# Windowed attention of chunks 2 to 8 on 64x64 TensorE tiles, in plain float32, with the transposes first

## The chip, the cores and the metric

The kernel runs on one core of one Trainium2 chip. The metric is the device time of one execution in microseconds: the median of three runs. One more execution was recorded by the hardware profiler, and every duration below comes from that record. The engines are TensorE (PE for its matmuls, PEld for its weight loads), VectorE (DVE), ScalarE (ACT), GpSimd (POOL) and SyncE (SP, which issues most of the DMAs).

## What is computed

Three stages follow one another: attention with a causal window of 128 and a linear bias, a dense gated feed-forward, and a mixture of eight experts that takes the best expert of each token.

```python
# q, k, v: [4, 8, 576, 64] float32; window = 128
scores = q @ k.T / sqrt(64)
rel = pos[:, None] - pos[None, :]
scores = where((rel >= 0) & (rel < 128), scores - slope[h] * abs(rel), -1e9)
attn = softmax(scores);  x = (attn @ v) as [2304, 512]
h = x @ w_in;  y = (h * clip(h + 3, 0, 6) / 6) @ w_out        # 512 -> 2048 -> 512
e = argmax(cosine(y, expert_emb) / tau)                        # 8 experts
out = gate * relu(y @ w1[e]) @ w2[e]                           # 512 -> 1024 -> 512
```

A query sees its own key and the 127 before it, so 64 queries that start at a multiple of 64 need 192 keys at most: the 128 before the block and the 64 of the block.

## The kernel before

The 2304 tokens are cut into nine **chunks** of 256. Attention is done in **units** of one chunk and one pair of heads, 36 in all. Chunks 0 and 1 (class `Early`) are worked off in a list that `plan()` writes ahead of time, together with the preparation of the feed-forward weights. Chunks 2 to 8 are 28 units of class `Unit`, and they are the ones that change.

What a `Unit` does, in order: `load` and `load_v` fetch keys, queries and values (SP's DMAs); `transpose_qk` turns keys and queries on DVE so that the 64 features of head 0 lie in partitions 0 to 63 and those of head 1 in 64 to 127; `split_qk` makes of each a high and a low part in the type fp32r (ACT and DVE); `scores` (L621) multiplies in three passes (high x high, high x low, low x high), for 128 queries by 256 keys at a time, one head in the upper half of TensorE's rows and one in the lower; `soften` adds the bias from `table`, takes the largest and the exponential; `normalise` divides; `flip_p` (L683) transposes the weights on TensorE against `ident`; `unload_p` copies them from PSUM (ACT) and splits them with two masks (POOL) into the part of the own key block and that of the block before; `values` (L723) multiplies by `vr` into one PSUM tile `acc`, head 0 in the left half of TensorE's columns, head 1 in the right; `keep_x` splits `acc` into the fp32r pair `xs` that the feed-forward reads. Where a chunk crosses the end of a sequence (every 576 tokens), the blocks have 64 rows, and there are more of them.

TensorE, ACT, DVE and SP work their instructions off in program order, and that order is set by numbers: `at(step, fn)` hangs a function on a step, and all are emitted by step (those of one step as they were entered). A group of attention work stands at `group(n)`, between two blocks of the feed-forward: the values of unit n-2, the flips of unit n-1 and the scores of unit n, in this order. `gemm1` (L750) and `gemm2` (L793) of the feed-forward lie around it, 24 matmuls of 128x128 by 256 columns and 12 by 512, all fp32r in three passes. PSUM has eight banks, handed out by the tile framework (`bank`).

At the very start POOL makes constants in program order: `whole` and `table` (the bias, L172 to L181), some others, and `units_of` (L215), the scale of the queries, which the first ACT instruction on queries (L439) reads.

A plain float32 matmul shows as two records in the trace, and a transpose or an fp32r matmul as one.

Of the kernel before, what the change touches and what calls it, by code (L numbers as in the profile page):

```python
# [19 lines left out]
MASKED = -1.0e32  # L20
# [37 lines left out]
P_BUFS, V_BUFS = 2, 2  # L58

# [31 lines left out]
def tile_kernel(  # L91
# [89 lines left out]
    nc.gpsimd.tensor_copy(out=table, in_=whole)  # L181

# [153 lines left out]
    def segments(c):  # L336

        qs, ks = [], []
        g, end = c * CH, (c + 1) * CH
        while g < end:  # L340
            b, s = divmod(g, S)
            n = min(S - s, end - g)
            prev = None
            if s:
                h = min(128, s)
                ks.append((b, s - h, h))
                prev = len(ks) - 1
            for o, m in runs(n):
                ks.append((b, s + o, m))
                qs.append((b, s + o, m, len(ks) - 1, prev))  # L350
                prev = len(ks) - 1
            g += n
        return qs, ks


# [170 lines left out]
    class Unit:  # L526
        def __init__(self, n):
            self.c, self.p = divmod(n, NP)
            self.h0 = 2 * self.p
            self.qs, self.ks = segments(self.c)  # L530
            self.koff = [sum(x[2] for x in self.ks[:j]) for j in range(len(self.ks) + 1)]
            self.qoff = [sum(x[2] for x in self.qs[:j]) for j in range(len(self.qs) + 1)]
            self.soff = [0]
            for _, _, m, _, prev in self.qs:
                self.soff.append(self.soff[-1] + m + (self.ks[prev][2] if prev is not None else 0))


            self.width, self.wins = {}, []
            col = 0
            for full in (True, False):  # L540
                for j, (_, _, m) in enumerate(self.ks):
                    if (m == 128) == full:
                        users = [i for i, x in enumerate(self.qs) if x[3] == j]
                        users += [i for i, x in enumerate(self.qs) if x[4] == j]
                        w = sum(self.qs[i][2] for i in users)
                        self.wins.append((j, m, col, w, users))
                        col += w
                self.width[full] = col
            self.own, self.prev = {}, {}
            for j, _, at, _, users in self.wins:  # L550
                for i in users:
                    (self.own if self.qs[i][3] == j else self.prev)[i] = at
                    at += self.qs[i][2]

            befores = {x[4] for x in self.qs}
            self.row = [128 - x[2] if j in befores else 0 for j, x in enumerate(self.ks)]
            self.even = all(x[2] == 128 and x[4] is not None and self.ks[x[4]][2] == 128 for x in self.qs)
            self.pt, self.sm, self.pp = {}, {}, {}
        def load(self):
            def get_blocks(src, blocks, off, nm):  # L560

                t = raw.tile([128, off[-1] // 32, 32], F32, tag=nm, name=nm)
                j = 0
                while j < len(blocks):
                    b, s, n = blocks[j][:3]
                    j0 = j
                    j += 1
                    while j < len(blocks) and blocks[j][0] == b and blocks[j][1] == s + n:
                        n += blocks[j][2]
                        j += 1  # L570
                    for h in range(2):
                        for f in range(2):
                            nc.sync.dma_start(
                                out=t[64 * h + 32 * f:64 * h + 32 * f + 32, off[j0] // 32:(off[j0] + n) // 32, :],
                                in_=src[b, self.h0 + h, s:s + n, 32 * f:32 * f + 32].rearrange("(t j) i -> j t i", j=32),
                            )
                return t

            self.kr = get_blocks(k, self.ks, self.koff, "kr")
            self.qr = get_blocks(q, self.qs, self.qoff, "qr")  # L580

        def load_v(self):
            t = raw.tile([128, len(self.ks), 128], F32, tag="vr", bufs=V_BUFS, name="vr")
            for j, (b, s, n) in enumerate(self.ks):
                nc.sync.dma_start(
                    out=t[self.row[j]:self.row[j] + n, j, :].rearrange("p (h d) -> p h d", h=2),
                    in_=v[b, self.h0:self.h0 + 2, s:s + n, :].rearrange("h p d -> p h d"),
                )
            self.vr = t

        def transpose_qk(self):
            def turn(src, width, nm):
                t = at2.tile([128, width], F32, tag=nm, bufs=1, name=nm)
                V.transpose(out=t, in_=src.rearrange("p t i -> p (t i)")[:, 0:width])
                return t

            self.kT = turn(self.kr, self.koff[-1], "kT")
            self.qT = turn(self.qr, CH, "qT")

        def split_qk(self):  # L600
            nk, sc = self.koff[-1], units_of[:, self.p:self.p + 1]
            self.k1 = k1 = at2.tile([128, 2, 384], F32R, tag="k1", bufs=1, name="k1")
            self.q1 = q1 = at2.tile([128, 2, CH], F32R, tag="q1", bufs=1, name="q1")
            nc.scalar.activation(out=q1[:, 0, :], in_=self.qT, func=AF.Copy, scale=sc)
            V.scalar_tensor_tensor(
                out=q1[:, 1, :], in0=self.qT, scalar=sc, in1=words(q1[:, 0, :]), op0=ALU.mult, op1=ALU.subtract
            )
            split(k1[:, 0, 0:nk], k1[:, 1, 0:nk], self.kT[:, 0:nk])

        def blocks(self):  # L610
            for j, (_, _, n, kj, prev) in enumerate(self.qs):
                first = kj if prev is None else prev
                yield j, n, self.koff[first], self.koff[kj], self.koff[kj + 1], self.soff[j], self.soff[j + 1]

        def scores(self):
            self.sc = [bank([128, 512], "sc_ps") for h in range(2)]
            for j, n, c0, cm, c1, s0, s1 in self.blocks():
                for x, (a, b) in enumerate(PASSES):
                    for h in range(2):
                        r = slice(64 * h, 64 * h + 64)  # L620
                        nc.tensor.matmul(  # L621
                            self.sc[h][0:n, s0:s1], lhsT=self.q1[r, a, self.qoff[j]:self.qoff[j] + n],
                            rhs=self.k1[r, b, c0:c1], start=(x == 0), stop=(x == 2),
                        )

        def soften(self, h):
            slope = 2.0 ** -(self.h0 + h + 1)
            pt = at2.tile([128, 512], F32, tag="p", bufs=P_BUFS, name="pt")
            nm = at2.tile([128, 4], F32, tag="nm", name="nm")
            sm = sums[h]  # L630
            for j, n, c0, cm, c1, s0, s1 in self.blocks():

# [924 lines left out]
```

## Time and profile before

| | us |
|---|---|
| median of 3 runs | 806.35 (806.11 to 807.45) |
| the profiled execution | 805.95 |
| its span, first to last instruction | 804.2 |
| PE busy | 782.9 (97%) |
| DVE / ACT / POOL busy | 476.0 / 410.3 / 152.5 |

The profiled execution's span is 1.75 us shorter than its own time, and its time lies 0.4 us under the median. The stretches are: to about 100 us the early attention and the weights' preparation, from there to about 515 us the feed-forward with the attention of chunks 2 to 8 between its blocks, and then the experts. In a list in order of time, the difference between the starts of two neighbouring rows of one engine is what the first of them takes on that engine: matmuls are pipelined, so a row's own length reaches into the next.

### The profile page before, as it was taken

The page shows a single profiled execution, that of the slowest core. Times are in us where ns is not written, and L with a number is a line of the kernel's source. Part 1 is how long each engine was busy: PE and PEld are TensorE (multiplying, and loading weights), DVE is VectorE, ACT ScalarE, POOL GpSimd, SP SyncE. Part 2 cuts the span into 40 slices and gives each one's busy share as a digit, 9 for nine tenths or more (in the row PEclk, how much of TensorE's full clock was granted, in tenths as well). Part 3 has the DMA queues.
Part 4 walks back from the last instruction along what each step waited for, and adds up shares of the span by engine and source line. Part 5 has one row for each costly group of instructions (what it writes and reads, how often), then busy time and mean ns, then how long its engine had stood idle before and what let it go on. Part 6 is the DMA issues. An engine that isn't in the chain of part 4 may idle for free.

```text
span 804.2 us, 15466 instructions
## 1 busy us (share of the span) xinstructions
PE 782.9 (97%) x5618; PEld 684.5 (85%) x5618; DVE 476.0 (59%) x1372; ACT 410.3 (51%) x1021; POOL 152.5 (19%) x279
## 2 busy tenths in 40 slices
PE   7999999999999999999999999999989999999995
PEld 5656587888888888888888888987989999999994
DVE  3899987765655646647547454247727547546620
ACT  7896676554544444555454453326626525535510
POOL 2000013112201113113121221013123132133200
PEclk9999999999999999999999999999999999999998
DMA  9965324433232132222222110029358565466200
GB/s 257 298 239 159 94 56 61 62 67 80 40 83 60 33 71 72 37 70 60 50 63 57 37 59 3 27 26 326 124 158 280 172 220 190 137 212 208 85 26 27
DMA packets 154834, 88.20 MB, mean 110 GB/s; under 512 B 116947, under 2 KB 133459, under 8 KB 154752
## 3 DMA queue, kind: packets, MB, share of 16 engines
q1 hardware_dynamic: 151008, 77.57, 34.6%
q0 software_dynamic: 3744, 9.58, 3.4%
q8 instruction: 46, 0.75, 0.4%
q14 instruction: 36, 0.29, 0.2%
HBM read 72.76 MB, written 14.46 MB: 108 GB/s over the span
## 4 chain that ended last, share of the span: by engine, by line
PE 80%; issue 6%; DVE 5%; ACT 4%; DMA 3%; POOL 1%; SPq 0%; POOLq 0%; DVEq 0%; ACTq 0%
PE y_ps L793 19%; PE h_ps L750 19%; PE ps_u L1039 12%; PE ps_o L1063 8%; PE acc L723 3%; PE sc_ps L621 3%; PE ps_z L1121 3%; PE y_ps L784 2%; PE ps_pt L683 2%; DMA slots<-pays,dest 2%; PE ps_x L1009 1%; ACT pt L469 1%; PE h_ps L737 1%; PE ps_z L1135 1%; ACT pt L485 1%
## 5 line engine op out<-in xcount | busy, mean ns | idle before, releaser
L750 PEld LDWEIGHTS h_ps<-xs,w_i 128*128 128x128 f32 x1536 | 191.6, 191 | 5.7 <-issue 0.5
L750 PE MATMUL h_ps<-xs,w_i 128*128 128x256 f32 x1536 | 195.6, 284 | 0.0
L793 PE MATMUL y_ps<-w_o,gh 128*128 128x512 f32 x512 | 163.7, 401 | 1.6 <-ACT gh L154 1.6
L760 ACT ACTIVATE u<-h_ps,three 128x512 f32<-128x512 f32 x72 | 49.3, 685 | 152.0 <-PE h_ps L750 124.7
L793 PEld LDWEIGHTS y_ps<-w_o,gh 128*128 128x128 f32 x512 | 91.5, 188 | 21.5 <-ACT gh L154 2.0
L767 DVE SCALAR_TENSOR_TENSOR u<-u,h_ps 128x512 f32<-128x512 f32 x72 | 49.2, 683 | 100.7 <-ACT u L760 97.4
L1039 PE MATMUL ps_u<-x,w_e 128*128 128x280 f32 (+5 forms) x768 | 105.0, 293 | 0.0
L793 PE MATMUL y_ps<-w_o,gl 128*128 128x512 f32 x256 | 100.4, 392 | 0.4 <-DVE gl L155 0.4
L1039 PEld LDWEIGHTS ps_u<-x,w_e 128*128 128x128 f32 x768 | 100.1, 188 | 0.2
L155 DVE TENSOR_TENSOR w_e<-st,w_e 128x1024 fp32r<-128x1024 f32 x64 | 76.4, 1216 | 38.2 <-ACT w_e L154 38.2
L1063 PE MATMUL ps_o<-hs,w_e 128*128 128x280 f32 (+4 forms) x576 | 79.4, 297 | 0.0
L1063 PEld LDWEIGHTS ps_o<-hs,w_e 128*128 128x128 f32 x576 | 77.5, 190 | 0.0
L154 ACT CAST w_e<-st 128x1024 fp32r<-128x1024 f32 x64 | 65.6, 1050 | 17.2 <-DMA st<-in_moe_w_dram 6.1
L155 DVE TENSOR_TENSOR gl<-u,gh 128x512 fp32r<-128x512 f32 x64 | 46.2, 722 | 35.3 <-ACT gh L154 35.1
L696 POOL TENSOR_SCALAR_AFFINE_SELECT ph<-ph 128x256 f32<-128x256 f32 (+3 forms) x80 | 32.3, 412 | 157.7 <-ACT ph L693 151.8
L653 ACT ACTIVATE pt<-pt,nm 128x128 f32<-128x128 f32 (+2 forms) x128 | 49.8, 390 | 23.1 <-DVE pt L642 16.1
L793 PEld LDWEIGHTS y_ps<-w_o,gl 128*128 128x128 f32 x256 | 48.1, 188 | 12.3 <-DVE gl L155 1.5
L1138 POOL DMA_INDIRECT out_dram<-ob,ids x23 | 31.6, 1374 | 114.6 <-DVE ob L1137 103.8
L154 ACT CAST gh<-u 128x512 fp32r<-128x512 f32 x64 | 39.7, 620 | 20.5 <-DVE u L767 19.5
L1047 ACT ACTIVATE hs<-ps_u 128x280 fp32r<-128x280 f32 (+5 forms) x64 | 25.6, 403 | 44.6 <-PE ps_u L1039 40.5
L634 DVE CUSTOM_DVE_ANT_0 pt<-sc_ps,table 128x256 f32<-128x256 f32 (+3 forms) x128 | 41.9, 366 | 2.9 <-PE sc_ps L621 2.8
L1048 DVE SCALAR_TENSOR_TENSOR hs<-ps_u,hs 128x280 fp32r<-128x280 f32 (+5 forms) x64 | 27.9, 442 | 20.5 <-ACT hs L1047 20.2
(179 smaller groups left out, 1078.5 us busy)
## 6 DMA issues: line engine op xcount, KB each, us to landing
st<-in_moe_w_dram SPq DMA_DIRECT2D x32, 512.0 KB
st<-in_moe_w_dram SPq DMA_DIRECT2D x16, 1024.0 KB
wst<-in_moe_w_in_dram SPq DMA_DIRECT2D x8, 1024.0 KB
wst<-in_moe_w_out_dram SPq DMA_DIRECT2D x8, 1024.0 KB
vr<-in_v_dram SPq DMA_DIRECT2D x72, 64.0 KB
ybuf<-ys SPq DMA_DIRECT2D x18, 256.0 KB
out_dram<-empty SPq DMA_DIRECT2D x18, 256.0 KB
kr<-in_k_dram SPq DMA_DIRECT2D x48, 48.0 KB
```

The lines of the kernel that those rows point to most:

```text
L154: nc.scalar.copy(hi, src)
L155: eng.tensor_tensor(out=lo, in0=src, in1=words(hi), op=ALU.subtract)
L634: V.tensor_tensor_reduce(out=pt[0:n, s0:s1], in0=self.sc[h][0:n, s0:s1], in1=table[0:n, t0:t0 + c1 - c0], scale=-slope, scalar=3.0e38, op0 ...
L653: nc.scalar.activation(out=pt[0:n, a:a + m], in_=pt[0:n, a:a + m], func=AF.Exp, scale=-1.0, bias=nm[0:n, j:j + 1], accum_out=sm[0:n, j:j + 1],
L696: nc.gpsimd.affine_select(out=p[r0:r1], in_=o[r0:r1], compare_op=ALU.is_gt, fill=0.0, base=r0, pattern=dims + [[-1, o.shape[-1]]], channel ...
L750: nc.tensor.matmul(hp[:, f, :], lhsT=w[:, a, kk, f * 128:(f + 1) * 128], rhs=xs[:, b, kk, :], start=(n == 0), stop=(n == 3 * KD - 1),)
L760: nc.scalar.activation(out=u, in_=hp, func=AF.Relu, bias=three, scale=1.0)
L767: V.scalar_tensor_tensor(out=u, in0=u, scalar=6.0, in1=h_t[c, i], op0=ALU.min, op1=ALU.mult)
L793: nc.tensor.matmul(y_t[c][t], lhsT=g[a][:, f, t * 128:(t + 1) * 128], rhs=w[:, b, f, :], start=(i == 0 and f == 0 and n == 0), stop=(i == ...
L1039: nc.tensor.matmul(ps, lhsT=w[:, a, kk, (f % 2) * 128:(f % 2) * 128 + 128], rhs=x[:, b, kk, c0:c1], start=(n == 0), stop=(n == 3 * KD - 1),)
L1063: nc.tensor.matmul(ps, lhsT=ws_t[j, 4 + f // 2][:, a, f % 2, d * 128:(d + 1) * 128], rhs=hs[:, b, f, 0:width(j)], start=(n == 0), stop=(n ...
L1138: x = nc.gpsimd.indirect_dma_start(out=out, out_offset=bass.IndirectOffsetOnAxis(ap=ids[0:n, t, 0:1], axis=0), in_=ob[0:n], in_offset=None ...
```

## The change

- **Scores**: `split_qk` is gone; `scale_q` scales the turned queries in place (ACT). The scores are plain float32, on quarters of TensorE: 64 queries by 192 keys at a time, head in the row half, even or odd block of 64 queries in the column half. Eight matmuls of 192 columns for every unit, instead of 12 or 18.
- **Bias tables**: five of 128x192 (`tables`), cut from `whole` on POOL at the start: two copies each, and a mask where a block lies near the start of a sequence. The same shapes serve every unit, so the special cases for short blocks go.
- **Flips**: always four, 128x128, their output in two strips; and they and `unload_p` are hung 0.01 step earlier, ahead of the values in the same group.
- **Unload**: one copy for each head, and four masks of 64 partitions instead of two of 128.
- **Values**: even key blocks in the upper row half, odd ones in the lower, each half into a PSUM bank of its own; 12 matmuls on quarters. ACT then copies one bank (`part`), DVE adds the other (`both`), and `keep_x` splits `both`.
- **Value loads** are one head at a time: 2 to 8 DMAs in a unit instead of 3 or 4.

```diff
+    for kinds in ((2, 2), (2, 0), (2, 1), (1, 2), (0, 2)):
+        tables[kinds] = t = const.tile([128, 192], BF16, name="table%d%d" % kinds)
+        for h, kind in enumerate(kinds):
+            r = slice(64 * h, 64 * h + 64)
+            nc.gpsimd.tensor_copy(out=t[r], in_=whole[r, 64 * h:64 * h + 192])
+            if kind < 2:
+                nc.gpsimd.memset(t[r, 0:128 - 64 * kind], MASKED)
...
-        def split_qk(self):
...
+        def scale_q(self):
+            nc.scalar.activation(out=self.qT, in_=self.qT, func=AF.Copy, scale=units_of[:, self.p:self.p + 1])
...
-            self.sc = [bank([128, 512], "sc_ps") for h in range(2)]
-            for j, n, c0, cm, c1, s0, s1 in self.blocks():
-                for x, (a, b) in enumerate(PASSES):
-                    for h in range(2):
...
+            self.sc = [bank([128, 2, 192], "sc_ps") for h in range(2)]
+            for j in range(2):
+                for h in range(2):
+                    r = slice(64 * h, 64 * h + 64)
+                    for s in range(2):
+                        o = 64 * j + 128 * s
                         nc.tensor.matmul(
+                            self.sc[h][64 * s:64 * s + 64, j, :], lhsT=self.qT[r, o:o + 64], rhs=self.kT[r, o:o + 192],
...
-            acc = bank([128, CH], "acc")
...
+            accs = [bank([128, CH], "acc") for _ in range(2)]
+            for x, wins in enumerate((((2, 0, 0, 3), (3, 2, 1, 3)), ((4, 3, 2, 2), (1, 0, 0, 2)), ((0, 5, 0, 1), (5, 5, 3, 1)))):
+                for r, (y, at, m, n) in enumerate(wins):
+                    for h in range(2):
+                        nc.tensor.matmul(
+                            accs[r][64 * h:64 * h + 64, 64 * m:64 * (m + n)],
+                            lhsT=self.vr[64 * r:64 * r + 64, y // 2, 64 * h:64 * h + 64],
+                            rhs=self.pp[h][64 * r:64 * r + 64, at:at + n, :],
...
+            nc.scalar.copy(part, accs[1])
+            V.tensor_tensor(out=both, in0=accs[0], in1=part, op=ALU.add)
+            keep_x(self.c, self.p, both, V)
...
-        at(t0 - turn, u.split_qk)
+        at(t0 - turn, u.scale_q)
...
-        at(t1, u.flip_p)
+        at(t1 - FLIPS_AHEAD, u.flip_p)
         for h in range(2):
-            at(t1, u.unload_p, h)
+            at(t1 - FLIPS_AHEAD, u.unload_p, h)
```

TensorE, one group of the middle of the feed-forward, before (`h_ps` and `y_ps` are outputs of the feed-forward's two matmuls, `ps_y` is a transpose for the routing, `acc` the values, `ps_pt` the flips, `sc_ps` the scores; a shape is that of the output):

```order
L750 MATMUL h_ps<-xs,w_i 128x256 x24
L821 MATMUL ps_y<-ident,ys 128x128 x4
L723 MATMUL acc<-ph,vr 64x128 x2
L723 MATMUL acc<-ph,vr 64x256 x2
L723 MATMUL acc<-ph,vr 64x128 x2
L683 MATMUL ps_pt<-ident,pt 128x128 x4
L621 MATMUL sc_ps<-k_3775,q_3776 128x256 x12
L793 MATMUL y_ps<-w_o,gh 128x512 x2
```

The same group after:

```order
L676 MATMUL h_ps<-xs,w_i 128x256 x24
L747 MATMUL ps_y<-ident,ys 128x128 x4
L618 MATMUL ps_pt<-ident,pt 128x2x64 x4
L644 MATMUL acc<-ph,vr 64x192 x4
L644 MATMUL acc<-ph,vr 64x128 x4
L644 MATMUL acc<-ph,vr 64x64 x4
L583 MATMUL sc_ps<-kT,qT 64x192 x8
L719 MATMUL y_ps<-w_o,gh 128x512 x2
```

The flips moved ahead of the values, next to the full-size matmuls, and values and scores, now both on quarters, stand side by side.

POOL at the start of the program, before, from the table of the bias to the scale of the queries (`fixed`, 64x1 x8):

```order
L181 CAST table<-whole 128x256
L207 MEMSET ones 128x128
L208 MEMSET fixed 128x2
L209 MEMSET enT 128x128
L215 MEMSET fixed 64x1 x8
```

After:

```order
L182 CAST table<-whole 128x256
L188 CAST table_100<-whole 64x192 x2
L188 CAST table_103<-whole 64x192 x2
L188 CAST table_107<-whole 64x192
L190 MEMSET table_103 64x128
L188 CAST table_107<-whole 64x192
...
L188 CAST table_115<-whole 64x192 x2
L190 MEMSET table_115 64x128
L216 MEMSET ones 128x128
L217 MEMSET fixed 128x2
L218 MEMSET enT 128x128
L224 MEMSET fixed 64x1 x8
```

Ten copies and four masks now stand ahead of the scale of the queries.

ACT around one group, before (`u` and `gh` belong to the feed-forward, `xs<-acc` is the copy of the values, `ph` the unload, `q` and `k` the split for the next unit, the last two the exponentials):

```order
L760 ACTIVATE u<-h_ps,three 128x512
L154 CAST xs<-acc 128x256
L693 COPY ph<-ps_pt 128x2x128
L154 CAST gh<-u 128x512
L693 COPY ph<-ps_pt 128x2x128
L604 ACTIVATE q_3776<-qT,fixed 128x256
L154 CAST k_3775<-kT 128x384
L653 ACTIVATE pt,sums_131<-pt,nm 128x128 x2
L653 ACTIVATE pt,sums_132<-pt,nm 128x128 x2
```

After:

```order
L686 ACTIVATE u<-h_ps,three 128x512
L625 COPY ph<-ps_pt 128x2x128 x2
L155 CAST gh<-u 128x512
L652 COPY part<-acc 128x256
L155 CAST xs<-both 128x256
L602 ACTIVATE pt,sums_150<-pt,nm 128x128 x2
L602 ACTIVATE pt,sums_151<-pt,nm 128x128 x2
L574 ACTIVATE qT<-qT,fixed 128x256
```

The copy of `k` is gone, `part` is new, and the copy to `xs` now stands behind `part` and waits for DVE's sum `both`.

## Rows read from the trace of the kernel before

**Rows 1.** Page, part 1: busy time, share of the span, instructions of each engine.

```profile
PE 782.9 (97%) x5618; PEld 684.5 (85%) x5618; DVE 476.0 (59%) x1372; ACT 410.3 (51%) x1021; POOL 152.5 (19%) x279
```

**Rows 2.** Stretches: length, busy PE PEld DVE ACT POOL (instructions), clock, DMA share, GB/s.

```profile
80.00:100.00 20.00, 18.64 (x68) 11.84 (x65) 19.72 (x21) 13.40 (x15) 0.00 (x0) 1.00 0.34 103
...
160.00:200.00 40.00, 40.00 (x294) 35.05 (x294) 25.55 (x96) 19.93 (x57) 7.43 (x14) 1.00 0.34 76
```

**Rows 3.** Waits of PE from 100 to 515 us: total, times, longest.

```profile
PE y_ps L793 <- ACT gh L154: 0.8, 1, 0.8
```

**Rows 4.** Groups by line, 100 to 510 us: busy us, mean ns, idle before.

```profile
L723 PE MATMUL acc<-ph,vr 128*64 128x128 f32 (+5 forms) x368 | 30.2, 295 | 0.0
L621 PE MATMUL sc_ps<-k,q 64*128 64x256 f32 (+4 forms) x384 | 28.2, 279 | 0.0
L683 PE MATMUL ps_pt<-ident,pt 128*128 128x128 f32 (+1 forms) x128 | 22.6, 283 | 0.0
```

**Rows 5.** In order of time (start us, us, engine, line, operation): one attention group.

```profile
300.77 1.09 PE L723 MATMUL acc<-ph,vr 128*64 128x128 f32 x12
301.79 0.66 PE L683 MATMUL ps_pt<-ident,pt 128*128 128x128 f32 x4
302.37 0.98 PE L621 MATMUL sc_ps<-k,q 64*128 64x256 f32 x12
303.28 0.74 PE L793 MATMUL y_ps<-w_o,gh 128*128 128x512 f32 x2
```

**Rows 6.** PE in order of time: 24 full-size matmuls, ahead of the same and another shape.

```profile
154.33 3.03 PE L750 MATMUL h_ps<-xs,w_i 128*128 128x256 f32 x24
157.29 0.50 PE L723 MATMUL acc<-ph,vr 128*64 128x64 f32 x6
...
313.03 3.03 PE L750 MATMUL h_ps<-xs,w_i 128*128 128x256 f32 x24
315.90 0.18 PE L876 MATMUL rk<-oh,earlier 128*128 128x16 bf16 x1
```

**Rows 7.** PE in order of time: an early unit's flips, plain float32 scores and values.

```profile
60.80 0.60 PE L492 MATMUL ps_pt<-ident,pt 128*128 128x128 f32 x4
61.33 1.14 PE L447 MATMUL sc_ps<-kt,qt 64*128 64x256 f32 x8
62.40 1.09 PE L505 MATMUL acc<-ph,stage 128*64 128x128 f32 x12
63.41 0.91 PE L737 MATMUL h_ps<-xf,w 128*128 128x256 f32 x3
```

**Rows 8.** PE in order of time: routing on four column quarters, and what follows.

```profile
306.27 0.64 PE L840 MATMUL lgT<-yT,enT 128*32 128x128 f32 x16
306.84 0.39 PE L750 MATMUL h_ps<-xs,w_i 128*128 128x256 f32 x1
```

**Rows 9.** POOL and ACT in order of time, at the start.

```profile
2.92 0.39 POOL L181 CAST table<-whole 128x256 bf16<-128x256 f32 x1
3.27 0.20 POOL L207 MEMSET ones<- 128x128 bf16 x1
...
3.58 1.07 POOL L215 MEMSET fixed<- 64x1 f32 x8
...
5.51 0.37 ACT L434 COPY kt<-ps_qk 128x256 f32<-128x256 f32 x1 [3.22 <-PE ps_qk L425]
5.78 0.48 ACT L439 ACTIVATE qt<-ps_qk,fixed 128x256 f32<-128x256 f32 x1
```

**Rows 10.** The chain that ended last, in order of time: start us, us, what.

```profile
5.89 0.39 ACT qt L439
...
93.92 7.13 PE y_ps L784 x16
```

**Rows 11.** All engines in order of time, 213 to 226 us: end of a chunk's attention.

```profile
216.58 0.42 DVE L155 TENSOR_TENSOR xs<-acc,xs 128x256 fp32r<-128x256 f32 x1
...
220.34 3.04 PE L750 MATMUL h_ps<-xs,w_i 128*128 128x256 f32 x24
```

More of the change, by code (lines that the diff above doesn't have):

```diff
@@ L334, in tile_kernel, with pieces_of, table_of @@
     x_t = {}
-    def segments(c):
-        qs, ks = [], []
-        g, end = c * CH, (c + 1) * CH
+    def pieces_of(g, n):
+        out, end, o = [], g + n, 0
         while g < end:
[L341 to L353, printed above, removed]
+            b, at = divmod(g, S)
+            m = min(S - at, end - g)
+            out.append((b, at, o, m))
+            g, o = g + m, o + m
+        return out
+    def table_of(c, j):
+        return tables[tuple(min((c * CH + 64 * j + 128 * s) % S // 64, 2) for s in range(2))]
     assert S >= EARLY_CHUNKS * CH
@@ L529, in __init__, with get @@
             self.h0 = 2 * self.p
[L530 to L558, printed above, removed]
-        def load(self):
[L560 to L570, printed above, removed]
+            self.pt, self.pp = {}, {}
+        def load(self):
+            def get(src, g, n, nm):
+                t = raw.tile([128, n // 32, 32], F32, tag=nm, name=nm)
+                for b, s, o, m in pieces_of(g, n):
                     for h in range(2):
@@ L651, in soften @@
-            for j, n, *_ in self.blocks():
-                a, m = self.joint(j)
+                    out=pt[:, 192 * j:192 * j + 192], in0=self.sc[h][:, j, :], in1=table_of(self.c, j),
+                    scale=-slope, scalar=3.0e38, op0=ALU.add, op1=ALU.min, accum_out=nm[:, j:j + 1],
+                )
+            w = pt.rearrange("p (b k) -> p b k", k=64)
+            V.tensor_tensor(out=w[:, 0:6:5, :], in0=w[:, 0:6:5, :], in1=w[:, 2:4, :], op=ALU.min)
+            for j in range(2):
+                x = pt[:, 256 * j:256 * j + 128]
@@ L677, in flip_p @@
+            V.reciprocal(out=rs[:, 0:2], in_=rs[:, 0:2])
+            for j in range(2):
+                x = self.pt[h][:, 256 * j:256 * j + 128]
+                V.tensor_scalar(out=x, in0=x, scalar1=rs[:, j:j + 1], scalar2=None, op0=ALU.mult)
         def flip_p(self):
@@ L696, in part @@
+            for r, here, there in ((0, slice(0, 4, 3), slice(5, 1, -3)), (1, slice(1, 5, 3), slice(2, 6, 3))):
+                x, y = (pp[64 * r:64 * r + 64, z, :] for z in (here, there))
+                own, prev = (x, y) if r == 0 else (y, x)
+                for out in (y, x):
                     nc.gpsimd.affine_select(
-                        out=p[r0:r1], in_=o[r0:r1], compare_op=ALU.is_gt, fill=0.0, base=r0,
-                        pattern=dims + [[-1, o.shape[-1]]], channel_multiplier=1,
-                    )
```

137 lines of the change are left out of this document (41 added, 96 removed).

## The prediction

> **What bounds the kernel now.** The page's first part comes first: TensorE is busy for 97% of the span, DVE for 59%, ACT for 51%, POOL for 19% [rows 1]. That is a mean over unlike stages, so the table by stretch comes next. Between 80 and 100 us DVE is busy for 19.72 of 20 us and TensorE isn't full; from 160 to 200 us TensorE is busy for all of 40.00, at a granted clock of 1.00 (2.4 GHz), while DVE has 14 us to spare and ACT 20 [rows 2]. The waits say the same: from 100 to 515 us TensorE waits once for another engine, 0.8 us [rows 3]. So in the stretch that holds all 28 changed units, the end is set by what stands on TensorE, and each microsecond taken off there is a microsecond gained, as long as nothing makes TensorE wait.
>
> How much of it is attention? The three lines of values, scores and flips are busy for 30.2, 28.2 and 22.6 us, 81.0 together [rows 4]. Matmuls are pipelined, so the end of each run lies under the start of the next: in the group at 300.77 the values start 1.02 us ahead of the flips, these 0.58 ahead of the scores, and these 0.91 ahead of the feed-forward, 2.51 in all [rows 5]. Added from start to start in this way, the 28 units take **73.2 us**, 2.6 each; those with short blocks lie above 2.51.
>
> **Turning TensorE round.** A fixed cost hides in there. 24 full-size matmuls take 2.87 us when the next one has their shape (313.03 to 315.90) and 2.96 when attention on half the columns follows (154.33 to 157.29) [rows 6]: leaving a tile shape costs 0.09 us, about 0.1 below. Before, a group leaves a shape four times: feed-forward, values, flips, scores. The first of these lies ahead of the group, outside the 73.2: about 25 times 0.09, 2.2 us.
>
> **The flips.** Ahead of the values they follow full-size matmuls of the same shape. That case is in the trace: four flips behind full-size matmuls and ahead of another shape, from 60.80 to 61.33, **0.53 us**, the way out included [rows 7]. 28 times: 14.8 us.
>
> **The scores.** Plain float32 on two row halves: eight records of 256 columns take 1.07 us, 61.33 to 62.40 [rows 7]. These are four rounds of two that run together, at 2 cycles of 2.4 GHz a column (0.213 us a round, 0.85 in all), and 0.21 for weights of 128 columns and the way out. After, a unit has sixteen records of 192 columns. If the four quarters run together, that is four rounds of 0.16, 0.64 us; with the way out, 0.1, and the stagger of four starts, 0.02, **0.76**. 28 times: 21.3.
>
> **The values.** Pairs on column halves: 1.01 us for twelve records, 62.40 to 63.41 [rows 7], 0.85 of it columns. After: 24 records, in rounds of 192, 128 and 64 columns, each twice: 384 columns, twice, 0.64 us on four quarters, and 0.05 for the first weights. The scores behind them have the same shape, so there is no way out: **0.69**. 28 times: 19.3.
>
> That four quarters run together no row shows: the nearest are two row halves (above), and four column quarters at once: sixteen records of 128 columns in 0.57 us, 306.27 to 306.84 [rows 8], which is four rounds of 0.107 and 0.14 around them. One by one they would take 1.7. Rows and columns are free of each other as far as these rows go; the two row halves write into different PSUM banks in the changed code, as they do in the early units. So I take four at once as the value; the other end is two at once, twice the 0.64.
>
> Together after: 14.8 + 21.3 + 19.3 = 55.4, and 0.3 for the four groups at the ends that have only one or two parts: 55.7. Before: 73.2 + 2.2 = 75.4. **TensorE gains 19.7 us.**
>
> **POOL at the start.** This is where the change costs. The scale of the queries is written by eight small masks from 3.58 us on; the first ACT instruction on queries needs the second of them, ready at about 3.8 (1.07 us for eight, one every 0.14), and starts at 5.78, when the copy of the keys, begun at 5.51, lets it [rows 9]. So there are 2.0 us of slack. Now ten copies of 192 columns and four masks stand ahead. A copy of 256 columns keeps POOL for 0.35 us (2.92 to 3.27); three masks, two of 128 columns and one of 2, keep it from 3.27 to 3.58, so one of 128 about 0.14 [rows 9]. By columns a copy costs 0.29, between 0.20 and 0.39: 2.9 us (2.0 to 3.9); four masks 0.5 (0.4 to 0.8). The scale comes 3.4 us later (2.4 to 4.7), the queries start at 7.2 in place of 5.78: **+1.4 us** (0.4 to 2.7). This instruction is a piece of the chain that ended last (5.89), and that chain reaches, through ACT and then DVE, the matmuls at 93.92 from which TensorE is never free again [rows 10]. So I count the delay in full.
>
> **The other engines.** ACT loses a copy of 384 columns and gains `part`; DVE loses the two subtractions of the split and gains a sum; both have room [rows 2]. POOL has eight masks of half the partitions instead of four; the values that need them come a whole group later, some 14 us, and it is busy for 19% [rows 1]. SP's value loads number more or fewer by a few, for units whose loads are issued a group ahead. I cost these at nothing. Two waits are new. `scores` takes the last free PSUM banks: by the order of the program, the one for head 1 is freed by the gate of the feed-forward block before the last, or by the copy of a routing transpose; both end before TensorE has done flips and values (1.2 us). And the way from the values to `xs` grows by `part` and the sum. Before, the last pair's `xs` is done at 217.00, and the next chunk's first matmul starts at 220.34, 3.3 us later [rows 11]. The two steps are of the size of the existing one, 0.4 us each; with the bias work of DVE, which now stands between, 2 us at most. Cover remains, about 1 us; without it, seven chunks would each lose what is over.
>
> **The sum.** 805.95 - 19.7 + 1.4 = 787.65 for the profiled execution; the median of the runs lies 0.4 above it: **788.0 us**, 2.3% faster.
>
> **Rivals.**
>
> *Quarters run two at a time.* If quarters in different row halves and different columns shut each other out, values and scores stream 2 x 1.28 us instead of 2 x 0.64. A unit pays 1.28 more, 28 units 36: 788 + 36 = **824**, slower. For it: no row shows four quarters. Against it: halves of rows and quarters of columns each run at their full number [rows 7, 8]. The point from which it decides: the gain is 18.3 us over 28 units, 0.65 each, so the 1.28 us of streaming in a unit may grow to 1.93, that is 2.65 at a time, before the change loses.
>
> *Four quarters give less than four.* If weight loads or starts of forty records a unit hold them to about three at a time, streaming takes 1.71 us instead of 1.28, 0.43 more in a unit, 12 in all: **800**. For it: the change turns 24 records in a whole unit of rows 5 (scores and values) into 40, with a weight load each. Against it: sixteen records on four column quarters lost nothing [rows 8]. The Trainium skill bears on it: "TensorE: Matmul & The Clock Gate", section on packing small matmuls, has a table in which four row tiles came out 3.07 times as fast as one. By that table alone the time would be 788 + 28 x 1.28 x (4/3.07 - 1), about 799, called an estimate. The trace doesn't show it for columns: four rounds of 0.107 is all that the sixteen records leave room for [rows 8].
>
> *The gain is taken back by waits.* In-order ACT and DVE could be late with `gh`, `xs` or a bank; the single wait of 0.8 us [rows 3] shows that the feed-forward's own chain has limits. If half of the groups lost 0.4 us: 28 x 0.2 = 5.6, **794**.
>
> *The queries aren't late*, because the copies are cheap: 786.6.
>
> **Chances.** Four at once with little else, 784.5 to 791: 0.78 (the last rival is part of it). Waits, 791 to 797: 0.07. Three at a time, 797 to 804: 0.06. Slower: 0.07. Near nothing: 0.02. The range takes in the bounds of the delay at the start (-1.0, +1.3), a percent or so in the 55.7, and reaches to the waits: **784.3 to 795**. About 0.2% (1.6 us) is what a measurement of this kernel can tell from no change: faster 0.91, the same 0.02, slower 0.07.
>
> **What would show it.** Right: a group from flips to feed-forward takes about 2.0 us instead of 2.5 to 3.0; in it the flips 0.53, values 0.69, scores 0.76; the matmuls of four quarters start within 0.03 us of each other; queries start at about 7.2; the matmuls of 93.92 start at about 95.3; TensorE has no new waits from 100 to 500 us. Wrong: values and scores at 1.3 us each (pairs), the queries' delay regained by 94 us, or TensorE waiting for `part`, `both` or masks.

## The result and the profile after

The changed kernel takes **794.8 us** in the median of four runs (791.2 to 795.9) against 806.2 before: ratio 0.985, 95% interval 0.983 to 0.986. Five more runs of it gave 792.1 (791.1 to 794.3), ratio 0.983 (0.981 to 0.985). The forecast was 788.0, range 784.3 to 795: the direction held and the time lay at the upper end of the range. By the first median 11.4 us came of the 18.3 that were forecast, by the second 14.1. The profiled execution takes 795.89, its span is 793.9.

The first part of its page, columns as in [rows 1], shows the work that went (TensorE 783 to 769 us) and POOL's that came (22% in place of 19%):

```profile
PE 769.2 (97%) x5970; PEld 677.6 (85%) x5970; DVE 454.7 (57%) x1272; ACT 400.5 (50%) x941; POOL 177.1 (22%) x357
```

One attention group in order of time, the same place as [rows 5]:

```profile
300.05 0.60 PE L618 MATMUL ps_pt<-ident,pt 128*128 128x128 f32 x4
300.58 0.89 PE L644 MATMUL acc<-ph,vr 64*64 64x192 f32 x24
301.29 0.83 PE L583 MATMUL sc_ps<-kT,qT 64*64 64x192 f32 x16
302.05 0.73 PE L719 MATMUL y_ps<-w_o,gh 128*128 128x512 f32 x2
```

Flips 0.53, values 0.71, scores 0.76, together 2.00 us in place of 2.51: the forecast was 0.53, 0.69 and 0.76. From 160 us on, every group reads like this one. So the missing time is elsewhere, and two places show it.

**The start.** POOL and ACT in order of time, as in [rows 9]; the last line is the row that answers to 93.92 of [rows 10]:

```profile
3.27 1.90 POOL L188 CAST table<-whole 64x192 bf16<-64x192 f32 x5
...
7.00 0.74 POOL L188 CAST table<-whole 64x192 bf16<-64x192 f32 x2
...
8.27 0.39 POOL L224 MEMSET fixed<- 64x1 f32 x3
8.54 0.47 ACT L439 ACTIVATE qt<-ps_qk,fixed 128x256 f32<-128x256 f32 x1 [2.65 <-POOL fixed L224]
97.40 4.99 PE L710 MATMUL y_ps<-w,u 128*128 128x512 f32 x11 [1.36 <-DVE w L320]
```

The tables keep POOL from 3.27 to 7.94, the queries start at 8.54 in place of 5.78, and TensorE's full stretch begins at 97.40 in place of 93.92: 3.5 us, not 1.4.

**The first groups of chunk 2.** The waits of PE from 100 to 515 us (total, times, longest), as in [rows 3], and the stretch from 140 to 160 us (columns as in [rows 2]):

```profile
PE ps_pt L618 <- DVE pt L612: 1.7, 3, 1.0
PE acc L644 <- POOL ph L633: 0.4, 1, 0.4
140.00:160.00 20.00, 18.63 (x165) 15.71 (x158) 12.26 (x48) 9.42 (x30) 5.10 (x16) 0.91 0.43 54
```

Before there was one wait, of 0.8 us; the new ones are for the softmax (DVE) and for the masks (POOL). They look small, since PE counts as busy while a pipelined matmul drains, and while matmuls run at a lower clock, as they do below. The group of the second unit, at 126 us, DVE and PE in order of time:

```profile
123.14 0.24 DVE L795 TENSOR_SCALAR rn<-rn 128x2 f32<-128x2 f32 x1 [2.38 <-POOL rn L759]
...
126.56 0.43 PE L618 MATMUL ps_pt<-ident,pt 128*128 128x128 f32 x2 [0.37 <-DVE pt L612]
127.40 0.53 PE L618 MATMUL ps_pt<-ident,pt 128*128 128x128 f32 x2 [0.40 <-DVE pt L612]
127.85 1.05 PE L644 MATMUL acc<-ph,vr 64*64 64x192 f32 x24
```

DVE stands 2.4 us at a small step of the router that waits for POOL, and the unit's softmax is queued behind it. Flips, now first in their group, wait for that softmax. The group takes 3.04 us in place of 2.00, and TensorE is idle for 0.4 us ahead of it.

The group at 146 us, all engines:

```profile
140.10 0.28 POOL L633 TENSOR_SCALAR_AFFINE_SELECT ph<-ph 64x128 f32<-64x128 f32 x1 [2.61 <-ACT ph L625]
...
146.37 0.69 ACT L686 ACTIVATE u<-h_ps,three 128x512 f32<-128x512 f32 x1 [1.76 <-remote]
...
146.69 0.38 PE L618 MATMUL ps_pt<-ident,pt 128*128 128x128 f32 x2
146.87 5.72 POOL L633 TENSOR_SCALAR_AFFINE_SELECT ph<-ph 64x128 f32<-64x128 f32 x15 [6.48 <-DMA slots<-pays,dest]
...
148.03 0.53 PE L618 MATMUL ps_pt<-ident,pt 128*128 128x128 f32 x2 [0.96 <-DVE pt L612]
148.49 0.54 PE L644 MATMUL acc<-ph,vr 64*64 64x192 f32 x2
...
149.43 1.24 PE L644 MATMUL acc<-ph,vr 64*64 64x192 f32 x19 [0.41 <-POOL ph L633]
...
152.31 0.58 PE L676 MATMUL h_ps<-xs,w_i 128*128 128x256 f32 x1
```

POOL does one mask at 140.10 and then stands still for 6.5 us, until the two scatters of the router (issued at 135.0 and 136.5) have landed. The other seven masks of that unit begin at 146.87, and its values, next in TensorE's queue, have to wait for them. The flips of the second head wait too: ACT is late by 1.8 us for something that the profile calls "remote", so DVE's gate is, and the normalisation behind it. From 146.69 to 152.31 the group takes 5.62 us. Behind the idle time the granted clock falls to 1.2 GHz (0.51 in the mean of 150 to 153 us, same columns as above), and the feed-forward matmuls run slowly until about 153.5: the 24 at 152.31 take 3.47 us up to 155.78, where the 24 at 140.96 took 2.97, so 0.5 us more.

```profile
150.00:153.00 3.00, 3.00 (x37) 2.34 (x30) 1.21 (x5) 1.16 (x4) 2.13 (x8) 0.51 0.13 27
```

Where the wait for the scatters is set shows in the order of POOL's instructions in the built program; DMASW are the semaphores on which the two scatters report:

```
55 L818 DMA slots<-pays,dest 20480x2 [waits DMAHW3_49,DVE_49,Pool_49]
56 L818 DMA slots<-pays,dest 20480x2
57 L633 AFFINE_SELECT ph<-ph 64x2x64 [waits Activation_49]
58 L633 AFFINE_SELECT ph<-ph 64x2x64 [waits DMASW1_49,DMASW0_49]
```

The first mask on partitions 64 to 127 behind every pair of scatters waits for them. The mask reads and writes nothing of the scatters' data (`ph` against `pays`, `dest` and `slots`); why the build puts the wait there stays open. Before, the masks covered all partitions from 0 on in this chunk, and only the next chunk's scatter waited. But in one later chunk of that kernel a mask on partitions 64 to 127 did wait in the same way, at 442 us, and the trace from which the prediction was made has the line (waits of POOL from 95 to 520 us; total, times, longest):

```profile
POOL ph L696 <- DMA slots<-pays,dest: 4.7, 1, 4.7
```

In the changed kernel this happens in all seven chunks, 39.7 us of POOL in all, up to 7.4 at a time. In the later ones the groups stand 13 to 15 us apart and nobody notices; here the next group comes 7.7 us behind.

### The profile page after: what moved, and what is told of

Its sections match the earlier page's. It is cut to its first block, busy times and chain, and to the rows that moved or that the text cites. A ratio compares the mean times of both kernels' runs of the same rounds, so it can differ in the third digit from the quotient of the medians.

```text
span 793.9 us, 16238 instructions
## 1 busy us (share of the span) xinstructions
PE 769.2 (97%) x5970; PEld 677.6 (85%) x5970; DVE 454.7 (57%) x1272; ACT 400.5 (50%) x941; POOL 177.1 (22%) x357
## 5 line engine op out<-in xcount | busy, mean ns | idle before, releaser
L633 POOL TENSOR_SCALAR_AFFINE_SELECT ph<-ph 64x128 f32<-64x128 f32 x224 | 78.1, 349 | 141.3 <-ACT ph L625 88.7
L602 ACT ACTIVATE pt<-pt,nm 128x128 f32<-128x128 f32 x112 | 44.1, 394 | 31.3 <-DVE pt L599 29.9
L974 DVE SCALAR_TENSOR_TENSOR hs<-ps_u,hs 128x280 fp32r<-128x280 f32 (+5 forms) x64 | 27.9, 442 | 20.1 <-ACT hs L973 19.8
L818 POOL DMA_INDIRECT slots<-pays,dest x18 | 19.9, 1104 | 84.6 <-DVE u L693 52.1
```

The source lines that it names most:

```text
L602: nc.scalar.activation(out=x, in_=x, func=AF.Exp, scale=-1.0, bias=nm[:, j:j + 1], accum_out=sums[h][:, j:j + 1])
L633: nc.gpsimd.affine_select(out=out, in_=x, compare_op=ALU.is_gt if out is prev else ALU.is_ge, fill=0.0, base=0, pattern=[[0, 2], [-1 if ou ...
L974: V.scalar_tensor_tensor(out=hs[:, 1, f, c0:c1], in0=ps, scalar=0.0, in1=words(hs[:, 0, f, c0:c1]), op0=ALU.max, op1=ALU.subtract)
```

## The experiments

The readings that bear on all of them, from each profiled execution (us): the start of the row that answers to 93.92; the time from there to the start of the last values of attention (494.42 in the changed kernel, 505.16 before); the groups at 126 and 146 from their first attention matmul to the feed-forward behind them; and the median of the runs with its ratio to the kernel before.

| kernel | full stretch from | to last values | group 126 | group 146 | median | ratio (95%) |
|---|---|---|---|---|---|---|
| before | 93.92 | 411.2 | | | 806.2 | |
| changed | 97.40 | 397.0 | 3.04 | 5.62 | 794.8 | 0.983 to 0.986 |
| changed_again | 98.80 | 394.7 | 3.04 | 3.72 | 792.1 | 0.981 to 0.985 |
| tables_late | 94.43 | 394.5 | 3.04 | 3.58 | 787.7 | 0.977 to 0.979 |
| before_with_tables | 96.77 | 411.2 | | | 807.7 | 1.001 to 1.005 |
| scatter_later | 97.40 | 393.5 | 3.05 | 2.48 | 790.5 | 0.980 to 0.984 |
| no_odd_masks | 97.46 | 394.4 | 3.05 | 2.94 | | |
| softmax_first | 97.43 | 392.7 | 2.65 | 2.65 | 788.8 | 0.977 to 0.982 |
| late_and_scatter | 94.12 | 393.5 | 3.05 | 2.49 | 788.4 | 0.976 to 0.980 |
| late_scatter_softmax | 94.01 | 392.6 | 2.65 | 2.49 | 786.7 | 0.974 to 0.978 |
| flips_last | 97.43 | 401.8 | 3.25 | 3.88 | 798.8 | 0.990 to 0.993 |
| quarter_by_quarter | 97.47 | 422.4 | | | 821.9 (one run) | |

**1. The tables behind the scale of the queries.** The block that makes the tables, moved:

```
     nc.gpsimd.tensor_copy(out=table, in_=whole)
-    tables = {}
-    ...
...
     nc.gpsimd.iota(iota_e, pattern=[[1, NE]], ...)
+    tables = {}
+    ...
```

> The changed kernel, with the fourteen POOL instructions that make the tables moved behind the scale of the queries and the last small constant; nothing else moves. Theory (the start): the delay of the queries, 8.54 in place of 5.78 us, goes through the whole first stretch, so that the down matmuls which begin TensorE's full stretch stand at 97.40 in place of 93.92. With the tables behind, queries start at about 5.8, that row stands at about 93.9, and the time falls by about 3.5 us, to 791.3. Rival (the delay is partly taken up by something else that is late by then, weights from memory for one): the queries start at 5.8 but the row stands at 95.5 or later, and the time falls by less than 2 us, to 793 or above.

ACT and PE in order of time, three places:

```profile
6.03 0.48 ACT L439 ACTIVATE qt<-ps_qk,fixed 128x256 f32<-128x256 f32 x1
...
94.43 7.13 PE L710 MATMUL y_ps<-w,u 128*128 128x512 f32 x16 [1.36 <-DVE w L320]
...
145.79 0.87 PE L644 MATMUL acc<-ph,vr 64*64 64x192 f32 x18 [0.28 <-POOL ph L633]
```

The rows do nearly what the theory says: the full stretch starts 3.0 us earlier, of 3.5. The time falls by 7.1 (4.4 against the second median of the changed kernel), which is more than the start gives. In this execution the scatters land 10.7 us after the issue of the first, not 11.9, the clock doesn't fall behind the group at 146, and that group loses 2.0 us less; and what follows attention is 2.2 us shorter (297.3 for 299.5), which this edit doesn't touch (see the end). So the start is worth 3 us, and the second loss isn't a fixed one.

**2. The tables alone, on the kernel before.** Their fourteen instructions, put where the change has them, into tiles that nothing reads:

```
+    for kinds in ((2, 2), (2, 0), (2, 1), (1, 2), (0, 2)):
+        t, n = spare[n % 2], n + 1
+        ...
```

> The kernel before with ten copies of 64 rows by 192 columns and four masks on POOL where the change makes its tables, written by turns into two tiles that nothing reads; all attention as before. Theory (the start by itself): the queries start at about 8.5 in place of 5.78 us, the down matmuls of 93.92 stand at about 97, and the time grows by 3.0 to 3.5, to about 809.5. Rival (only the 1.4 us of the prediction arrive, the rest of the delay is regained before 94 us): 807.6.

```profile
8.61 0.47 ACT L450 ACTIVATE qt<-ps_qk,fixed 128x256 f32<-128x256 f32 x1 [2.72 <-POOL fixed L226]
...
96.77 5.42 PE L795 MATMUL y_ps<-w,u 128*128 128x512 f32 x12 [1.36 <-DVE w L322]
```

The queries are late by 2.83 and the full stretch by 2.85: the delay goes through undiminished, and the time to the last values is that of before. The interval of the ratio is 0.8 to 3.6 us, which holds both theories; the rows decide, not the time. The changed kernel's 3.5 has 0.6 more, which stands in its first scores: 1.65 us, where they take 0.93 here. Those rows, and the stretch from 8 to 12 us of run 3 (columns as in [rows 2]):

```profile
9.07 1.65 PE L447 MATMUL sc_ps<-kt,qt 64*128 64x128 f32 x8 [3.16 <-ACT qt L439]
9.14 0.93 PE L458 MATMUL sc_ps<-kt,qt 64*128 64x128 f32 x8 [3.23 <-ACT qt L450]
8.00:12.00 4.00, 2.94 (x15) 2.29 (x16) 1.13 (x8) 1.27 (x4) 1.41 (x16) 0.61 1.20 275
```

In runs 3 and 6 the first scores take the same 1.65 us, and there the granted clock is 0.50 (1.2 GHz) from 9 to 12 us (0.61 in the mean of the row above), after TensorE has stood idle for over 3 us waiting for the queries. Here it falls only at about 9.9, when the scores are nearly done. The profile of the changed kernel records no fall in that stretch, so for that execution the lower clock is inferred from the equal 1.65 us. The second execution (run 5) has 0.50 once more, from 16 to 19 us, and its second scores and the values behind them take 1.63 and 1.55 us in place of 0.93 and 0.87: that is why its full stretch begins at 98.80. So a late start can cost clock as well, from nothing (here) to 2 us (run 5), and that differs from execution to execution.

**3. The scatters behind the masks.** The router's `ranks` and `place` of the first chunk, two steps of the plan later:

```
-        at(g + d[3], r.ranks)
-        at(g + d[3], r.place)
+        d3 = d[3] + (2.0 if c == 0 else 0)
+        at(g + d3, r.ranks)
+        at(g + d3, r.place)
```

> The changed kernel, with the routing of the first chunk (ranks, slots and POOL's two scatters) two steps of the plan later, so that the two scatters stand behind the masks of the next two groups and not ahead of them. Theory (the scatter's landing): at 140 to 147 us POOL waits 6.5 us in the middle of the masks until the scatters have landed, values of the group at 146.5 wait for these masks, and TensorE's clock falls to 1.2 GHz behind it. With the scatters behind the masks that group takes 3.3 us at most in place of 5.6, the granted clock stays at 1.00, and the time falls by about 3 us, to 791.8. Rival (the softmax of crowded groups is late, with or without masks): flips of that group still wait for DVE, and the time falls by less than 1 us, to 794 or above.

POOL and PE in order of time:

```profile
140.08 2.99 POOL L633 TENSOR_SCALAR_AFFINE_SELECT ph<-ph 64x128 f32<-64x128 f32 x8 [8.63 <-ACT ph L625]
...
146.73 0.60 PE L618 MATMUL ps_pt<-ident,pt 128*128 128x128 f32 x4
147.26 0.89 PE L644 MATMUL acc<-ph,vr 64*64 64x192 f32 x24
148.40 0.88 PE L583 MATMUL sc_ps<-kT,qT 64*64 64x192 f32 x16 [0.25 <-ACT qT L574]
```

All eight masks run at once, the group takes 2.48 us, the clock stays at 1.00 there. 3.5 us are gained on the way to the last values (1.2 against changed_again), 4.3 in the time (1.6 against the second median). The rival falls. ACT's wait of 1.8 us is gone as well, which the theory didn't say.

**4. The scatters where they were, and no mask that waits for them.** In `unload_p`:

```
+                if r:
+                    nc.scalar.copy(y, x)
+                    continue
```

> The changed kernel without the masks of the odd key blocks: POOL's four masks of a unit on partitions 64 to 127 are left out, and ACT copies the two blocks that they would have written (two copies more a unit); so its values are not those of attention. No other POOL instruction waits for the landing of a scatter then, and the scatters stay where they are, ahead of the masks. Theory (the scatter's landing, through the masks on the upper partitions, is what held the values at 146.5): POOL no longer waits for the scatters, values of that group take 0.7 us as everywhere, and the time falls by 2 to 3, to about 792, whatever else that group waits for; if ACT is late there again (1.8 us in the changed kernel) the flips still wait. Rival (the masks are late because everything in that stretch is, and the wait for the scatters hides nothing): the group still takes over 4 us, and the time stays at 794 or above.

```profile
147.27 0.60 PE L618 MATMUL ps_pt<-ident,pt 128*128 128x128 f32 x4
147.79 0.89 PE L647 MATMUL acc<-ph,vr 64*64 64x192 f32 x24
149.39 0.88 PE L583 MATMUL sc_ps<-kT,qT 64*64 64x192 f32 x16 [0.71 <-ACT qT L574]
```

Values follow flips at once, and POOL has no wait for a scatter in the whole stretch. The group takes 2.94 us, of which 0.7 is a wait of the scores for the queries, behind ACT's extra copies. With other values of attention the router sends tokens elsewhere and what follows attention is another program (2126.5 us), so only the rows up to the last values are compared: 2.7 us gained (0.3 against changed_again, where the group lost less, and since this kernel loses 0.5 us ahead of the group). With run 3 this settles that the values waited for the masks and the masks for the scatters.

**5. The same kernel again.**

> The changed kernel once more, unchanged, with another profile: its runs lay between 791.2 and 795.9. Theory (the loss at 146.5 depends on when the scatters land among the loads of that stretch, and comes and goes from run to run): the runs spread by 3 us or more again, and the group at 146.5 takes another time than 5.6 us, with POOL's wait for the scatters shorter or longer by as much. Rival (it is fixed by the order of the program): 5.6 us again within 0.3, and the spread of 4.7 us is from elsewhere.

```profile
147.49 5.79 POOL L633 TENSOR_SCALAR_AFFINE_SELECT ph<-ph 64x128 f32<-64x128 f32 x15 [5.68 <-DMA slots<-pays,dest]
...
148.65 0.54 PE L644 MATMUL acc<-ph,vr 64*64 64x192 f32 x2
150.04 1.00 PE L644 MATMUL acc<-ph,vr 64*64 64x192 f32 x19 [0.85 <-POOL ph L633]
```

POOL waits 0.8 us less, ACT's "remote" wait and the fall of the clock aren't there, and the group takes 3.72 us. So the loss isn't fixed: 1.7 us here, and 1.9 and the 0.5 of the feed-forward behind the group more in the first profile. There the masks go on 0.18 us behind the group's first flip, here 0.64 ahead of it, which is 0.8 of the 1.9; the other 1.1 is that from 150 us on values and scores themselves ran at the lower clock. The late flips of the first profile hide behind the masks, since the values still waited 0.41 us for these after them. What ACT waited for there stays open. A slow fetch of instructions doesn't explain it by itself: the one block fetched in that stretch takes 1.2% of 16 engines' 15 us, 2.9 us, in the first profile and 0.2%, 0.5 us, in run 3, but 1.1%, 2.6 us, in this execution, in which ACT doesn't wait.

**6. The router's norms behind the softmax.** One dependence more in `choose`, `first` being the first step on the logits:

```
-            V.tensor_scalar(out=rn, in0=rn, scalar1=1e-6, ...)
+            x = V.tensor_scalar(out=rn, in0=rn, scalar1=1e-6, ...)
+            tc.add_manual_dep(x.ins, first.ins.name, PLACED, ...)
```

> The changed kernel with one dependence more: DVE's two small steps on the norms of the router stand behind the first step on the logits, and so no longer ahead of the softmax of the second unit. In the changed kernel DVE waits there 2.4 us for POOL (120.8 to 123.1), with that softmax queued behind, and the flips at 126 wait for it. Theory (that is what the group at 126 lost): its flips take 0.53 us in place of 1.3 and start 0.4 us earlier; the time falls by 1.2 to 1.5, to 793.4. Rival (the values behind them wait for masks or for the bank instead, and the next groups take it back): less than 0.5 us, 794.5.

DVE and PE in order of time:

```profile
122.38 0.36 DVE L593 CUSTOM_DVE_ANT_0 pt<-sc_ps,table 128x192 f32<-128x192 f32 x1 [1.58 <-PE sc_ps L583]
...
126.08 0.97 PE L618 MATMUL ps_pt<-ident,pt 128*128 128x128 f32 x4
126.98 1.05 PE L644 MATMUL acc<-ph,vr 64*64 64x192 f32 x24
```

The softmax starts 1.1 us earlier (122.38 for 123.50), the idle time ahead of the flips is gone and the group takes 2.65: 0.8 us of the 1.2 to 1.5 expected, since the flips are still a little late. But the way to the last values is 4.3 us shorter (2.0 against changed_again), because what stands behind comes earlier too: the scatters are issued at 134.15 for 135.01 and POOL goes on at 143.10 for 146.87, ahead of the next group. The time falls by 6.0 us by the medians (3.3 against the second) and by 7.7 between the profiled executions; what the way doesn't give lies behind attention, which this edit doesn't touch (296.2 us for 299.5, see the end). The expectation was right in place and sign and too small.

**7. All of it.**

> Both of the above together: tables behind the scale of the queries, scatters of the first chunk behind the masks. If both theories hold and nothing else comes late in their place, the gains add up: 3.5 + 3, about 788.3, which is what the prediction gave with other terms. If the groups of the first attention chunk only find another thing to wait for (the second head's normalisation), 790 to 791.

> All three together: tables behind the scale of the queries, scatters of the first chunk behind the masks, norms behind the logits. If the three groups' losses are what stood between 788 and the measured time, the two late groups now take about 2.0 and 2.5 us and the time is 785.5 to 786.5. Rival (with the first two the third finds nothing left to gain): 787.5 to 788.5, as with the tables alone.

```profile
94.01 7.13 PE L710 MATMUL y_ps<-w,u 128*128 128x512 f32 x16 [1.36 <-DVE w L320]
...
144.12 0.88 PE L583 MATMUL sc_ps<-kT,qT 64*64 64x192 f32 x16 [0.27 <-ACT qT L574]
```

The first two together give 788.4, no less than the tables alone (787.7), though their last values stand 1.3 us earlier: what follows attention took 299.0 us here and 297.3 there (see the end). With the third, 786.7, ratio 0.976: the best of all, 8 us below the changed kernel's first median and 5 below its second. From the tables alone it can't be told by the time (the intervals overlap); by rows its attention ends 2.3 us earlier.

**8. Flips between values and scores,** as before: `FLIPS_AHEAD = 0.0`.

> The changed kernel with the flips back between values and scores, as they stood before; quarters, tables and masks stay. Theory (tile shapes): a group then leaves a shape four times in place of two, feed-forward, values, flips, scores; at 0.09 to 0.1 us each a steady group takes about 2.2 us in place of 2.0, 5 us over all. Against it the first groups of the first attention chunk, whose flips wait for the softmax (1.3 us at 126), gain up to 1 us, since flips come 0.7 us later. Together about 4 us more: 799. Rival (the order of flips and values doesn't matter, leaving a shape is hidden): a steady group stays at 2.0 us and the time is 793 to 795.

```profile
316.16 0.89 PE L644 MATMUL acc<-ph,vr 64*64 64x192 f32 x24
316.98 0.66 PE L618 MATMUL ps_pt<-ident,pt 128*128 128x128 f32 x4
317.57 0.88 PE L583 MATMUL sc_ps<-kT,qT 64*64 64x192 f32 x16
318.38 0.73 PE L719 MATMUL y_ps<-w_o,gh 128*128 128x512 f32 x2
```

2.22 us for 2.00: values 0.82 for 0.71, flips 0.59 for 0.53, scores 0.81 for 0.76. Each change of shape costs its 0.05 to 0.11 us, and the time is 798.8 where 799 was expected. The price of turning TensorE round, 0.09 us from [rows 6], was about right; "flips first" is worth 4 us (6.7 against the second median), with what it costs at 126 taken off. That the time met 799 so closely is partly luck: counted from the second median the same theory gives 796.

**9. Quarter by quarter.** The loops of `scores` and `values` turned over, so that one quarter's matmuls stand together:

```
-            for j in range(2):
-                for h in range(2):
-                    ...
-                    for s in range(2):
+            for h in range(2):
+                ...
+                for s in range(2):
+                    for j in range(2):
```

> The changed kernel with the same matmuls in another order: all of one quarter's scores one behind the other, then the next quarter's, and the same for the values. Theory (four at once comes from the order: matmuls start in the order written, and one waits until its own quarter is free): a quarter's four records of scores take 4 x 0.16 us by themselves and overlap the next quarter's only at their end, so scores take about 2.2 us in place of 0.76, values about 2.4 in place of 0.7, and the time is 795 + 28 x 3.1, about 880. Rival (TensorE takes later matmuls ahead of a quarter that is busy): nothing changes, 795. Pairs would give 824.

```profile
325.98 1.79 PE L644 MATMUL acc<-ph,vr 64*64 64x192 f32 x21
327.50 0.40 PE L583 MATMUL sc_ps<-kT,qT 64*64 64x192 f32 x3
327.61 0.33 PE L644 MATMUL acc<-ph,vr 64*64 64x128 f32 x2
...
328.57 0.73 PE L719 MATMUL y_ps<-w_o,gh 128*128 128x512 f32 x2
```

Values and scores take 2.59 us in place of 1.47. That is neither the strict order (4.6) nor no change: scores of three quarters, written behind all values, start at 327.50, ahead of the last three values, whose quarter is still busy. The changed kernel does the same in its slow group, where scores start at 150.27 and values written ahead of them at 150.47. So what stands near the start of this text, that TensorE works its instructions off in program order, doesn't hold from one quarter to another: later matmuls do go ahead of earlier ones, but not far: the values' next quarter starts 0.38 us behind the one before, when that one has begun three of its six records, while the scores, four records a quarter, run nearly all at once. My theory fell. For a kernel the lesson is only that quarters have to be written by turns: 27 us here against the changed kernel's first median. The Trainium skill, "TensorE: Matmul & The Clock Gate", section on packing small matmuls, says that matmuls start and end in program order; the starts in this trace differ (ends are modelled in a profile and show nothing here).

## Why the prediction was off

The time lies inside the stated range, 784.3 to 795, but at its edge, and that is partly luck: the prediction put 0.78 of its chances on 784.5 to 791, and the range reached to 795 for the rival of waits, which came out in another shape. One of its signs of being wrong came true as well, TensorE waiting for masks. And 1.6 us was too little for what a measurement can tell: the two medians of the changed kernel differ by 2.7.

**Right: the gain on TensorE.** With most waits taken away (run 7) the way from the full stretch's start to the last values is 411.2 - 392.6 = 18.6 us shorter, and its two slow groups still lose 0.65 and 0.5: 19.8 against 19.7 forecast. Flips and scores came out to the hundredth, values 0.02 longer. That the sum agrees so closely is luck in part, for two small errors cancel: from start to start the groups gain 0.9 us less than the 17.5 (73.2 - 55.7) of the forecast, and the rows between them 1.1 us more than its 2.2. Four quarters run at once, with starts 7 ns apart, in rounds of 0.16 us; the rivals of two and of three at a time are out. For three at a time the prediction named a table of the Trainium skill, "TensorE: Matmul & The Clock Gate", section on packing small matmuls, with 3.07 times for four row tiles; the trace shows no such loss for four quarters.

**Mis-sized: the start.** The term was +1.4 with bounds of 0.4 and 2.7; the queries came 2.76 late and the full stretch 3.5 (2.85 in run 2). The step that failed is the price of a copy "by columns". 192 columns on 64 partitions took 0.38 us (five in 1.90), no less than 256 on 128 partitions [rows 9], and the four memsets came with waits between them: 4.67 us in place of 3.4. The last part, that the delay counts in full, was right; what TensorE's clock does when it waits so long was not in the term at all (0.6 of the 3.5, see run 2). Together this is 2.1 us of the shortfall.

**Wrong: "I cost these at nothing".** The step on the other engines took the distance between groups, 14 us, from the later chunks and POOL's share from the mean [rows 1]. In chunk 2 two groups are 7.7 us apart. It also looked only at the masks' number, not at what each waits for; the order of POOL's instructions shows the wait for the scatters, and the trace of before had it once. And nowhere did it ask what late flips would cost: put first, they come a microsecond before the softmax is done at 126. These are the third rival, waits that take the gain back, with 794 and a chance of 0.07. It was sized at half of all groups with 0.4 us each; it was two groups with 1.4 and 4.1 us, 1.6 of the 4.1 at the lower clock. Together 5.5 us, in the profiled execution: 787.65 + 2.1 + 5.5 = 795.25, against 795.89; of the rest, 0.4 lies behind attention (299.5 us for 299.0).

**Right in passing:** `part`, `both`, the two banks and the bias work cost nothing that shows from 160 us on; the cover of about 1 us at the ends of chunks held.

## What to carry to other kernels

A share of 19% for an engine says nothing of the stretch in which its work is crowded: take distances and waits from the tightest place, and read for each moved or added instruction what its semaphore waits for, not only how many there are. On an in-order engine, a small instruction that waits (a scatter's landing, a router's norm) holds up everything behind it. Where a gain is forecast from many equal groups, look at the first ones by themselves.

## Not expected of the hardware

- Small POOL copies: 64 x 192 took 0.38 us, 128 x 256 took 0.35. Half the partitions and three quarters of the columns saved nothing.
- A scatter of 128 pairs of words took 9 to 12 us from the issue of the first of two to the landing of both while loads in packets of some 150 bytes ran (8.95, 10.7, 11.1 and 11.9 in four executions).
- Later matmuls start ahead of earlier ones on TensorE when they use another quarter (run 9).
- TensorE's granted clock falls for about 3 us between 570 and 595 us in the profiled executions of before, changed, scatter_later, late_and_scatter and flips_last, and between 605 and 610 in quarter_by_quarter, whose attention ends 25 us later; in that part of the program it doesn't in changed_again, tables_late, softmax_first, late_scatter_softmax and before_with_tables. From the start of the last values to the end of the span it is 298.2 to 300.1 us in the first six and 296.2 to 298.0 in the other five, whatever the change. 3 us at half the clock cost some 1.5, an estimate, so the fall needn't be all of the difference, and what brings it about isn't shown. That is up to 4 us of scatter between executions that doesn't follow the attention code, and why small differences were read from rows here and not from times.
